# Another order for the products of the gradient of w2, another pace of the side stream, tied edge copies and six store buffers

## The chip, the cores and the metric

The kernel runs on one core of a Trainium2 chip. A core has a matrix engine (TensorE, PE in the profile; PEld is its weight loads), a vector engine (VectorE, DVE), an activation engine (ScalarE, ACT), GpSimd (POOL) and SyncE (SP). Each runs its own queue of instructions in order and waits on semaphores; here SP issues loads and POOL issues stores to the DMA engines, besides some arithmetic on POOL. The metric is the device time in microseconds of one execution.

## The reference: a gated mix of two branches, and all its gradients

The reference takes `x` (2048 x 1024), computes the output and then, by the vector-Jacobian product with `grad_out`, the gradients of all inputs but `B_x`:

```python
g = sigmoid((x * gate_w).sum(-1, keepdims=True))
a = irfft2(rfft2(x) * (w_r + 1j * w_i))          # branch A, in fp32, cast to bf16
h = relu(einsum("bsd,df->bsf", x, w1) + b1) ** 2  # F = 3584
b = einsum("bsf,fd->bsd", h, w2) + b2
out = g * a + (1 - g) * b
```

The outputs are `out` and the gradients of `x`, `w_r`, `w_i`, `w1`, `b1`, `w2`, `b2` and `gate_w`.

## The kernel before

Two streams of work are woven into one program. The main stream is the dense branch B and its gradients; the side stream is the spectral branch A: a two-dimensional Fourier transform written as small matrix products, with its own gradients.

**The main stream** has five parts.

1. `mlp_in` (L701): for each of 28 blocks of 128 columns of `w1` and each of 4 blocks of 512 rows it makes the hidden values (`ph`, L726, 8 matmuls), evacuates them on ACT (L728, L729), makes the gradient with respect to the hidden values (`pd`, L736, 8 matmuls), and evacuates that on DVE (`dhT`, L740). One such pair is a unit. `later["last"]` is the latest `dhT` instruction written down. Both results are stored to DRAM (`h2T_scr`, `dhT_scr`).
2. The first part of `mlp_grads` (L828): the gradient of `w2`, as the product of the transposed hidden values with `dbn`, by Strassen and Winograd's scheme: seven products in place of eight for a block cut in quarters. There are 7 groups of 512 rows of the result (`FG`), two blocks to a group (`Block`, L908), so 14 blocks. A block has seven chains of eight matmuls, p1 to p7 (L918). They use the quarters of the left operand (a11, a12 from half 0 of the fetched tile, a21, a22 from half 1), sums S1 to S4 of these (`left`, L892; one DVE instruction each at L906), and sums T1 to T4 of the quarters of `dbn` (`right`, L878, once). Two accumulators in PSUM belong to a block: X collects p1, p6, p7, p4 in that order, and V holds p2, then p5 and p3. After p1, p6 and p7 X is copied by ACT (`c1`, `u2`, `u3`, L928); `wlo` and `whi` are the two rows of results: DVE adds V and `c1` after p2 (L939), V and `u3` after p7 (L951, `whi`), V and `u2` after p3 (L964); ACT copies X into `whi` after p4 (L959). p3 adds into V, so it may not start before the `whi` addition has read V. The left operand of group n is fetched by transposing DMAs on SP (`fetch`, L847, issued at L181) into one of two buffers, `even` and `odd`. S1 is written in place over a21.
3. The gradient of `w1`: 7 x 8 products `pw` (L1050) of 16 matmuls, evacuated by ACT into `wo` (L1052), which has three buffers (L1051), and stored by POOL (L1053).
4. `mlp_out` (L1085): the output of branch B, `acc` (L1133).
5. `GradOfX.products`: the gradient of `x`, again by seven products.

**The side stream** (`aside`, L1484) is a generator. Each `yield` ends a step: the rest of the first transform of `x`, that of the gradient, the middle stage `fft_mid` (L319) and the way back `fft_out` (L528). `fft_mid` first loads the edge columns of the spectrum (twelve small loads, L337 to L339), and writes out ten steps of which the first seven carry the summing of `dbn` over its 16 tiles (`sums_of_db`, L1465, the generator `filler`, two additions to a step), and then calls `edges_through` (L351): six small DVE copies of the edges, 32 small matmuls, and four copies. After it come 32 turns of four steps: a turn loads `z`, makes sums `pm` on DVE (not in the first pair), multiplies with a matrix (`px`, L414, two matmuls), copies the result to `x` with four ACT instructions (L417), multiplies with the filter on DVE (`tt`, L424, L425; the filter `w` is prepared on POOL, L392 and L398; `eh` at L430 to L433), recombines (`y`, L437, L438), transforms back (`pv`, L445, two matmuls; `pc`, L451, L452), and makes the gradients of the filter (L462 to L466, L470, L475), which are stored. `fft_out` makes 32 tiles in two steps each: a row is loaded (`r`, POOL), folded (`re` on ACT L551, `rf` on DVE L556, L557), multiplied (`pki`, L564), copied by ACT (`rt`, L566), multiplied (`pui`, L311), copied (`e`, L573, L574), recombined on DVE into `yo` (L590 to L592; two buffers) and stored to `ax_scr` (L593).

**The pace** is set by `spread` (L1369): each step of the main stream adds to a due count, and side steps are taken until the count is met. In `mlp_in` a unit adds 1.55 steps until the middle stage has begun, then 1.3 (`first_rate`, L1502), and nothing in the last four units. In the w2 part a chain adds half of 0.8 (`each` is 0.5, `rate`, L1512). In the gradient of `w1` each `pw` adds (todo - count) / 55, where `todo` is the number of side steps in all but the last 8 tiles (263) and `count` those already taken. The last tiles go beside `mlp_out`.

**The order in a queue** is not simply that of the program. The compiler's scheduler goes through its own estimate of time and lets an engine take the first instruction in program order that is ready by that estimate. `after(ins, earlier, NoSync)` (L235) fixes the order of two instructions of one engine without a wait. In the trace, S sums are seen ahead of instructions written down before them.

In one turn of the loop of the w2 part (L1004), block `b` is new and block `a` is the one before it, and the chains are written down in this order:

```python
b.p1(); a.p7(); b.p2(); b.p6(); a.p4(); a.p3(); b.p5()
```

The fetch of half 0 of group g + 2 stands after `b.p2` (of the second block of a group), the fetch of half 1 of group g + 1 after `a.p4` (of the first block). S4 of the group, or S3 and S1 of the next one, stand after `a.p3`, S2 of the next one after `b.p5`.

Of the kernel before, what the change touches and what calls it, by code (L numbers as in the profile page):

```python
# [10 lines left out]
P = 128  # L11
BF16 = mybir.dt.bfloat16
FP16 = mybir.dt.float16
FP32 = mybir.dt.float32
ALU = mybir.AluOpType
# [124 lines left out]
def kernel(  # L140
# [22 lines left out]
    nc = tc.nc  # L163
# [71 lines left out]
    def after(ins, earlier, wait=mybir.DependencyClass.Sync):  # L235

        if earlier is not None:
            info = mybir.DependencyInfo(wait, mybir.DependencyReason.DATA)
            tc.add_manual_dep(ins.ins, earlier.ins.name, info, reason="paced")
# [79 lines left out]
    def fft_mid(filler):  # L319
# [29 lines left out]
            return am.rearrange("p (m n q) -> p m n q", n=2, q=P)  # L349

        def edges_through(ams, ed, low, mid):  # L351
            nc.vector.tensor_copy(out=ed[lanes[0], :, 1, :], in_=ed[lanes[0], :, 0, :])
            nc.vector.tensor_copy(out=ed[lanes[0], 0, 1, :], in_=mid[lanes[0]])
            for n in range(2):
                a, b = slice(2 * n, 2 * n + 2), slice(2 - 2 * n, 4 - 2 * n)
                nc.vector.tensor_copy(out=ed[lanes[1], 1:, n, a], in_=low[lanes[1], 1:, a])
                nc.vector.tensor_scalar(out=ed[lanes[1], 1:, n, b], in0=low[lanes[1], 1:, b], scalar1=-1.0, scalar2=None, op0=ALU.mult)
            sp = fps.tile([P, NM, 2, 4], FP32, name="sp", tag="ps2", bufs=2)
            for h in range(2):
                for m in range(NM // 2):  # L360
                    for n in range(2):
                        mm(
                            sp[:, h * NM // 2 + m, n], lhsT=ams[h][:, m, n, :], rhs=ed[:, h * NM // 2 + m, n, :],
                            start=True, stop=True, skip_group_check=True,
                        )
            ex = fb.tile([P, NM, 2, 2, 2], FDT, name="ex", tag="ex")
            for n in range(2):
                for c in range(2):
                    nc.vector.tensor_copy(
                        out=ex[lanes[n], :, c], in_=sp[lanes[c], :, n, :].rearrange("p m (e t) -> p m t e", e=2)  # L370
                    )
            return ex
# [110 lines left out]
        turns = [(m, h) for m in range(NM) for h in (1, 0)]  # L483
        z = {0: inputs(*turns[0])}
        later["mid"] = True
        for n in range(10):
            if n < 7:
                next(filler, None)
            yield
        ex = edges_through(*edge)  # L490
        for _ in filler:
# [336 lines left out]
    def mlp_grads():  # L828
# [32 lines left out]
        def sums_of_b1():  # L861
            gb1 = wb.tile([P, FC], FP32, name="gb1", tag="gb1")
            behind(nc.vector.reduce_sum(out=gb1[:], in_=gb1part[:], axis=mybir.AxisListType.X), "DVE")
            gb1b = wb.tile([P, FC], BF16, name="gb1b", tag="gb1b")
            nc.vector.tensor_copy(out=gb1b[:], in_=gb1[:])
            pb1 = fps.tile([FC, P], BF16, name="pb1", tag="ps2", bufs=2)
            nc.tensor.transpose(pb1[:], gb1b[:], identb[:])
            gb1r = wb.tile([FC, P], BF16, name="gb1r", tag="gb1r")
            nc.vector.tensor_copy(out=gb1r[:], in_=pb1[:])
            st(out=out_5.rearrange("(fc p) -> fc p", p=P), in_=gb1r[:])  # L870
# [18 lines left out]
            V(out=T_[4], in0=b21, in1=T_[2], op=ALU.subtract)  # L889
            yield  # L890

        def left(g, *which):  # L892
            (a11, a12), (a21, a22) = quads(grp[g], FH)
            made = S_.setdefault(g, {})
            for n in which:
                if n == 1:
                    made[1] = fp16(a21)
                else:
                    made[n] = sb.tile([P, KH, FH], FP16, name=f"S{n}", tag=f"S{n}", bufs=2 if n == 3 else 1)[:]
                x, y, op = {  # L900
                    3: lambda: (a11, a21, ALU.subtract),
                    1: lambda: (a21, a22, ALU.add),
                    2: lambda: (made[1], a11, ALU.subtract),
                    4: lambda: (a12, made[2], ALU.subtract),
                }[n]()
                later["sum"] = V(out=made[n], in0=x, in1=y, op=op)  # L906

        class Block:  # L908

# [38 lines left out]
            def p7(self):  # L948
                self.chain(self.X, S_[self.g][3], T_[3], False)
                u3 = self.kept("u3")  # L950
                V(out=self.hi[:, H:D], in0=self.V[:], in1=u3[:], op=ALU.add)  # L951

            def store(self, part, i):
                f0 = self.g * FGW + i * FH + self.fb * P
# [36 lines left out]
        left(0, 4)  # L991
        fetch(2, 0)
        yield each
        blk[0].p7()
        next(sums)
        yield each
        blk[1].p6()
        yield each
        blk[0].p4()
        yield each  # L1000
        blk[0].p3()
        sums_of_b1()
        yield each
        for k in range(2, NB + 1):  # L1004
            a = blk.pop(k - 1)
            if k == NB:
                a.p7()
                yield each
                break
            g, second = divmod(k, 2)  # L1010
            b = blk[k] = Block(k)
            b.p1()
            if k == 2:
                left(1, 3, 1, 2)
            yield each
            a.p7()
            yield each
            b.p2()
            if second:
                fetch(g + 2, 0)  # L1020
            yield each
            b.p6()
            yield each
            a.p4()
            if not second:
                fetch(g + 1, 1)
            yield each
            a.p3()
            if not second:
                left(g, 4)  # L1030
            elif g + 1 < FG:
                left(g + 1, 3, 1)
            if k >= 6:
                more_of_x(3, a.last)
            yield each
            b.p5()
            if second and g + 1 < FG:
                left(g + 1, 2)
            yield each

        count = 0
        later["res1"] = True
        for n in range(FG, len(jobs)):
            cur = grp.pop(n)
            fg = jobs[n][1]
            for d_ in range(DC):
                pw = mps.tile([P, FGW], FP32, name="pw", tag=("pX", "pV")[count % 2], bufs=2)
                count += 1
                for t in range(NT):
                    mm(pw[:], lhsT=xr[:, t, d_ * P : (d_ + 1) * P], rhs=cur[:, t, :], start=(t == 0), stop=(t == NT - 1))  # L1050
                wo = wb.tile([P, FGW], BF16, name="wo1", tag="wo1", bufs=3)  # L1051
                nc.scalar.copy(out=wo[:], in_=pw[:])  # L1052
                st(out=out_4[d_ * P : (d_ + 1) * P, fg * FGW : (fg + 1) * FGW], in_=wo[:])  # L1053
                yield
                if n == FG and d_ == 0:
                    a.p4()
                    yield each
                    a.p3()
                    yield each
                    sbs.close()  # L1060
                    fetch(n + 1, 1)
                    high = later["w2high"] = db_p.tile([P, NT, D], BF16, name="w2high", tag="dbn")
                elif d_ == 0:
                    fetch(n + 1, 0, 1)
                if count % 2 == 0 and 4 <= count < NT + 4:
                    rows_of_w2(high, count - 4, 0)
# [398 lines left out]
    def sums_of_db():  # L1465
        kept = later["even"]
        acc = kept[:, 0 : 2 * D].bitcast(FP32)
        nc.vector.tensor_copy(out=acc, in_=dbn[:, 0, :])
        for n in range(1, NT):
            V(out=acc, in0=acc, in1=dbn[:, n, :], op=ALU.add)  # L1470
            if n % 2:
                yield
        tr_ = kept[:, 2 * D : 4 * D].bitcast(FP32)
        nc.vector.transpose(out=tr_, in_=acc)
        part = kept[:, 4 * D : 4 * D + 64].bitcast(FP32)
        nc.vector.reduce_sum(out=part, in_=tr_.rearrange("p (b r) -> p b r", r=32), axis=mybir.AxisListType.X)
        yield
        pr = fps.tile([32, 32], FP32, name="prow", tag="ps2", bufs=2)
        mm(pr[:], lhsT=part, rhs=sel[:], start=True, stop=True)
        row = kept[0:32, 4 * D + 64 : 4 * D + 96]  # L1480
        nc.vector.tensor_copy(out=row, in_=pr[:])
        st(out=out_7.rearrange("(b c) -> b c", c=32), in_=row)
# [18 lines left out]

    def first_rate():  # L1502
        left_[0] -= 1
        return 0.0 if left_[0] < 5 else 1.3 if "mid" in later else 1.55

    for _ in spread(units, spec, first_rate):
        pass
    grads = mlp_grads()
    next(grads), next(grads)
    todo = 22 + 2 * (NT + 4) + 10 + 3 + 4 * R1 + 2 + 8 + 2 * 25  # L1510

    def rate():  # L1512
        if "res1" not in later:
            return 0.8
        if "rate" not in later:
            later["rate"] = (todo - count[0]) / (FG * DC - 1.0)
        return later["rate"]
# [49 lines left out]
```

## Time and profile before

| What | Value |
|---|---|
| Median of six runs | 1263.02 us (1259.59 to 1265.4) |
| The six runs | 1265.40, 1265.36, 1260.12, 1259.59, 1260.95, 1265.09 us |
| The profiled execution: time, span | 1265.4 us, 1263.6 us |
| Busy in the span: PE, DVE, ACT, POOL | 1228.7, 784.1, 537.4, 372.6 us |
| `mlp_in` | up to 463 us |
| Gradient of w2 | 463 to 646 us |
| Gradient of w1 | 646 to 888 us |
| `mlp_out`, then the gradient of x | 888 to 1087, 1087 to the end |

A line of a timeline reads: start, duration, engine, line of the kernel, instruction, output <- inputs, shapes, number merged, and in brackets the idle time of that engine before it and what ended it. A line of waits reads: engine, tile and line that waited, what it waited for: total time, times, longest.

### The profile page before, as it was taken

How to read it: one execution, taken by the hardware profiler on the slowest of the kernel's cores; microseconds unless marked ns; L12 is line 12 of the kernel's file. 1: busy time of each engine (PE TensorE's matmuls, PEld its weight loads, DVE VectorE, ACT ScalarE, POOL GpSimd, SP SyncE). 2: the span in 40 equal slices, each digit the busy share in tenths (PEclk: the TensorE clock that was granted, in tenths of full speed). 3: DMA queues.
4: the chain of work that ended last, by engine and by line, in shares of the span. 5: the costliest groups of instructions: out<-in, count | busy, mean ns of one | idle time of the engine just before them, and what ended most of it. 6: DMA issues, size and time to landing. Idle time of an engine off the chain costs nothing.

```text
span 1263.6 us, 18788 instructions
## 1 busy us (share of the span) xinstructions
PE 1228.7 (97%) x6618; PEld 598.2 (47%) x6740; DVE 784.1 (62%) x1816; ACT 537.4 (43%) x1016; POOL 372.6 (29%) x616
## 2 busy tenths in 40 slices
PE   8999999999999999998999999899999999999998
PEld 5555555544444444443444445455544444444443
DVE  3556456567677768665767724455866555896573
ACT  4657667745767743333355635666311000011110
POOL 0124324332344412331346565666100000000000
PEclk9999999999999999998999999999999999999999
DMA  9567565666575858786889889997689867666520
GB/s 288 186 191 199 139 194 164 174 176 169 163 195 183 216 145 184 176 217 167 203 234 247 208 158 245 180 217 243 163 198 212 195 162 192 179 186 184 168 87 33
DMA packets 328728, 234.35 MB, mean 185 GB/s; under 512 B 197772, under 2 KB 283946, under 8 KB 328634
## 3 DMA queue, kind: packets, MB, share of 16 engines
q1 hardware_dynamic: 297680, 142.24, 48.9%
q0 software_dynamic: 30752, 90.87, 23.1%
q8 instruction: 52, 0.85, 0.3%
q14 instruction: 42, 0.34, 0.1%
q10 hardware_dynamic: 202, 0.04, 0.0%
HBM read 107.24 MB, written 81.81 MB: 150 GB/s over the span
## 4 chain that ended last, share of the span: by engine, by line
PE 48%; DMA 3%; DVE 2%; issue 1%; ACT 1%; POOL 0%; ACTq 0%; POOLq 0%; DVEq 0%
PE acc L1133 15%; PE pw L1050 12%; PE xX L1243 7%; PE xV L1243 3%; PE pX L918 3%; PE pV L918 3%; PE xZ L1243 2%; DMA out_dram<-wo 2%; PE pui L311 1%; PE pki L564 1%; DMA out_dram<-gw 1%; DMA ax_scr<-yo 0%; DVE dS L1230 0%; PE pv L445 0%; PE px L414 0%
## 5 line engine op out<-in xcount | busy, mean ns | idle before, releaser
L726 PE MATMUL ph<-xT,w1g 128*128 128x512 bf16 x864 | 214.8, 379 | 2.5 <-DMA w1g<-in_B_w_dram 0.7
L736 PE MATMUL pd<-dbT,w2T 128*128 128x512 bf16 x877 | 210.2, 379 | 3.3 <-DVE dhT L740 2.5
L740 DVE SCALAR_TENSOR_TENSOR dhT<-pd,rT 128x512 bf16<-128x512 f32 x112 | 77.0, 688 | 109.7 <-PE pd L736 100.2
L736 PEld LDWEIGHTS <-w2T 128*128 128x128 bf16 x896 | 87.1, 98 | 104.8 <-issue 3.1
L1050 PEld LDWEIGHTS <-res 128*128 128x128 bf16 x896 | 86.8, 98 | 100.0 <-issue 2.2
L726 PEld LDWEIGHTS <-w1g 128*128 128x128 bf16 x896 | 85.1, 98 | 92.6 <-DMA w1g<-in_B_w_dram 1.0
L1201 ACT ACTIVATE g<-gatew_bc,dsc 128x1024 f32<-128x1024 bf16 x16 | 18.3, 1147 | 255.9 <-DVE ot L1134 118.8
L1050 PE MATMUL pw<-odd,res 128*128 128x512 bf16 x499 | 114.5, 382 | 0.7
L728 ACT ACTIVATE rT<-ph,b1col 128x512 bf16<-128x512 f32 x112 | 77.1, 689 | 76.9 <-PE ph L726 76.0
L227 POOL DMA_DIRECT2D z_scr<-u x96 | 58.5, 616 | 107.5 <-ACT u L295 52.8
L417 ACT CAST x<-px 64x512 f16<-64x512 f32 x128 | 74.2, 580 | 27.3 <-PE px L414 26.2
L1050 PE MATMUL pw<-even,res 128*128 128x512 bf16 x374 | 84.6, 379 | 0.5
L227 POOL DMA_DIRECT2D r<-y_scr x96 | 58.2, 611 | 45.9 <-ACT re L551 14.0
L729 ACT ACTIVATE h2T<-rT 128x512 bf16<-128x512 bf16 x112 | 70.5, 629 | 2.3
L1243 PEld LDWEIGHTS <-dS 128*128 128x128 f16 x448 | 43.7, 98 | 53.4 <-DVE dS L1230 0.5
L1133 PEld LDWEIGHTS <-even 128*128 128x128 bf16 x448 | 43.6, 98 | 51.7
L1133 PEld LDWEIGHTS <-odd 128*128 128x128 bf16 x448 | 43.6, 98 | 51.4
L1134 DVE SCALAR_TENSOR_TENSOR ot<-acc,omg,af 128x512 bf16<-128x512 f32 x32 | 24.0, 750 | 67.5 <-PE acc L1133 63.3
L1052 ACT CAST wo<-pw 128x512 bf16<-128x512 f32 x56 | 32.7, 584 | 76.8 <-PE pw L1050 48.7
L1133 PE MATMUL acc<-w2high,odd 128*128 128x512 bf16 x251 | 57.4, 379 | 0.3
L1133 PE MATMUL acc<-w2high,even 128*128 128x512 bf16 x249 | 57.0, 379 | 0.3
L918 PEld LDWEIGHTS <-S 128*128 128x128 f16 x336 | 33.1, 99 | 47.0 <-issue 7.7
(226 smaller groups left out, 2143.1 us busy)
## 6 DMA issues: line engine op xcount, KB each, us to landing
h2T_scr<-h2T POOLq DMA_DIRECT2D x28, 512.0 KB, 4.1
dhT_scr<-dhT POOLq DMA_DIRECT2D x28, 512.0 KB, 5.6
z<-z_scr SPq DMA_DIRECT2D x64, 128.0 KB, 2.9
y_scr<-pc POOLq DMA_DIRECT2D x64, 128.0 KB, 3.6
ax_scr<-yo POOLq DMA_DIRECT2D x32, 256.0 KB, 5.0
w1g<-in_B_w_dram SPq DMA_DIRECT2D x14, 512.0 KB, 4.2
out_dram<-wo POOLq DMA_DIRECT2D x56, 128.0 KB, 5.6
even<-h2T_scr SPq DMA_DIRECT2D x8, 896.0 KB, 5.5
```

Source lines behind the costliest of these rows:

```text
L227: issue(out=a, in_=b) if stored else issue(out=b, in_=a)
L417: nc.scalar.copy(out=x[lanes[n], c, :, 0:HW], in_=px[lanes[c], n])
L726: mm(ph[:], lhsT=w1g[:, dc, fc % 2 * P : (fc % 2 + 1) * P], rhs=xT[:, dc, ss], start=(dc == 0), stop=(dc == DC - 1))
L728: nc.scalar.activation(rT[:], ph[:], ACT.Relu, bias=b1col[:, fc : fc + 1])
L729: nc.scalar.activation(h2T, rT[:], ACT.Square)
L736: mm(pd[:], lhsT=w_[:, ec, fc % FGC * P : (fc % FGC + 1) * P], rhs=dbT[:, ec, ss], start=(ec == 0), stop=(ec == DC - 1),)
L740: return STT(out=dhT, in0=pd[:], scalar=2.0, in1=rT[:], op0=ALU.mult, op1=ALU.mult, accum_out=gb1part[:, fc, sb : sb + 1],)
L918: self.mm = mm(acc[:], lhsT=lhs[:, t, c_], rhs=rhs[:, t, :], start=start and t == 0, stop=t == KH - 1, skip_group_check=True,)
L1050: mm(pw[:], lhsT=xr[:, t, d_ * P : (d_ + 1) * P], rhs=cur[:, t, :], start=(t == 0), stop=(t == NT - 1))
L1052: nc.scalar.copy(out=wo[:], in_=pw[:])
L1133: turn["PE"] = mm(acc[:], lhsT=cur[:, fc, t2 * P : (t2 + 1) * P], rhs=w2[fc // NT][:, fc % NT, cs], start=(fc == 0), stop=(fc == FC - 1))
L1243: mm(acc[:], lhsT=lhs[:, fc, :], rhs=rhs[:, fc, :], start=start and fc == 0, stop=fc == KH - 1, skip_group_check=True,)
```

## The change

Four things are changed.

- The chains of the w2 part are written down in the order `b.p1, b.p2, a.p4, b.p6, a.p3, b.p5, b.p7`: a block's p7 closes its own turn of the loop and is no longer in the turn of the next block. The last turn of the loop, which held only p7 of the last block, falls away. For the first two blocks the order becomes p6 of block 1, p7 of block 0, p7 of block 1, p4 and p3 of block 0. The S sums are written down after p7 (S4 of the group, or S3, S1 and S2 of the next group together), and each is tied behind the `whi` addition of that p7 on DVE without a wait.
- The six DVE copies of the edges are tied behind the latest `dhT`. The twelve steps ahead of them carry one step of the sums of `dbn` each; every addition of `sums_of_db` is now a step of its own, so the side stream has four steps more, and `todo` becomes 267.
- The pace in the first passes is 1.6 steps a unit in place of 1.3 once the middle stage has begun, and 0.9 in place of 0.8 in the w2 part.
- `wo1` has six buffers in place of three.

```diff
         def edges_through(ams, ed, low, mid):
-            nc.vector.tensor_copy(out=ed[lanes[0], :, 1, :], in_=ed[lanes[0], :, 0, :])
-            nc.vector.tensor_copy(out=ed[lanes[0], 0, 1, :], in_=mid[lanes[0]])
+            tied = lambda ins: after(ins, later["last"], mybir.DependencyClass.NoSync)
+            tied(nc.vector.tensor_copy(out=ed[lanes[0], :, 1, :], in_=ed[lanes[0], :, 0, :]))
+            tied(nc.vector.tensor_copy(out=ed[lanes[0], 0, 1, :], in_=mid[lanes[0]]))
...
-        for n in range(10):
-            if n < 7:
-                next(filler, None)
+        for _ in range(12):
+            next(filler, None)
             yield
         ex = edges_through(*edge)
...
-        def left(g, *which):
+        def left(g, *which, tie=None):
...
                 later["sum"] = V(out=made[n], in0=x, in1=y, op=op)
+                after(later["sum"], tie, mybir.DependencyClass.NoSync)
...
-                V(out=self.hi[:, H:D], in0=self.V[:], in1=u3[:], op=ALU.add)
+                self.added = V(out=self.hi[:, H:D], in0=self.V[:], in1=u3[:], op=ALU.add)
...
-        blk[0].p7()
+        blk[1].p6()
         next(sums)
         yield each
-        blk[1].p6()
+        blk[0].p7()
+        yield each
+        blk[1].p7()
         yield each
         blk[0].p4()
         yield each
         blk[0].p3()
         sums_of_b1()
+        left(1, 3, 1, 2, tie=blk[1].added)
         yield each
-        for k in range(2, NB + 1):
+        for k in range(2, NB):
             a = blk.pop(k - 1)
-            if k == NB:
-                a.p7()
-                yield each
-                break
             g, second = divmod(k, 2)
             b = blk[k] = Block(k)
             b.p1()
-            if k == 2:
-                left(1, 3, 1, 2)
-            yield each
-            a.p7()
             yield each
             b.p2()
             if second:
                 fetch(g + 2, 0)
             yield each
-            b.p6()
-            yield each
             a.p4()
             if not second:
                 fetch(g + 1, 1)
             yield each
+            b.p6()
+            yield each
             a.p3()
-            if not second:
-                left(g, 4)
-            elif g + 1 < FG:
-                left(g + 1, 3, 1)
             if k >= 6:
                 more_of_x(3, a.last)
             yield each
             b.p5()
-            if second and g + 1 < FG:
-                left(g + 1, 2)
             yield each
+            b.p7()
+            if not second:
+                left(g, 4, tie=b.added)
+            elif g + 1 < FG:
+                left(g + 1, 3, 1, 2, tie=b.added)
+            yield each
+        a = blk.pop(NB - 1)
...
-                wo = wb.tile([P, FGW], BF16, name="wo1", tag="wo1", bufs=3)
+                wo = wb.tile([P, FGW], BF16, name="wo1", tag="wo1", bufs=6)
...
             V(out=acc, in0=acc, in1=dbn[:, n, :], op=ALU.add)
-            if n % 2:
-                yield
+            yield
...
-        return 0.0 if left_[0] < 5 else 1.3 if "mid" in later else 1.55
+        return 0.0 if left_[0] < 5 else 1.6 if "mid" in later else 1.55
...
-    todo = 22 + 2 * (NT + 4) + 10 + 3 + 4 * R1 + 2 + 8 + 2 * 25
+    todo = 22 + 2 * (NT + 4) + 12 + 5 + 4 * R1 + 2 + 8 + 2 * 25
 
     def rate():
         if "res1" not in later:
-            return 0.8
+            return 0.9
```

More of the change, by code (lines that the diff above doesn't have):

```diff
@@ L351, in edges_through @@
         def edges_through(ams, ed, low, mid):
-            nc.vector.tensor_copy(out=ed[lanes[0], :, 1, :], in_=ed[lanes[0], :, 0, :])
-            nc.vector.tensor_copy(out=ed[lanes[0], 0, 1, :], in_=mid[lanes[0]])
+            tied = lambda ins: after(ins, later["last"], mybir.DependencyClass.NoSync)
+            tied(nc.vector.tensor_copy(out=ed[lanes[0], :, 1, :], in_=ed[lanes[0], :, 0, :]))
+            tied(nc.vector.tensor_copy(out=ed[lanes[0], 0, 1, :], in_=mid[lanes[0]]))
             for n in range(2):
                 a, b = slice(2 * n, 2 * n + 2), slice(2 - 2 * n, 4 - 2 * n)
-                nc.vector.tensor_copy(out=ed[lanes[1], 1:, n, a], in_=low[lanes[1], 1:, a])
-                nc.vector.tensor_scalar(out=ed[lanes[1], 1:, n, b], in0=low[lanes[1], 1:, b], scalar1=-1.0, scalar2=None, op0=ALU.mult)
+                tied(nc.vector.tensor_copy(out=ed[lanes[1], 1:, n, a], in_=low[lanes[1], 1:, a]))
+                tied(nc.vector.tensor_scalar(out=ed[lanes[1], 1:, n, b], in0=low[lanes[1], 1:, b], scalar1=-1.0, scalar2=None, op0=ALU.mult))
             sp = fps.tile([P, NM, 2, 4], FP32, name="sp", tag="ps2", bufs=2)
```

## Prediction

> **What bounds the kernel now.** I read the page first: the engine shares, then the slices.
>
> ```profile
> PE 1228.7 (97%) x6618; PEld 598.2 (47%) x6740; DVE 784.1 (62%) x1816; ACT 537.4 (43%) x1016; POOL 372.6 (29%) x616
> ...
> PE   8999999999999999998999999899999999999998
> ```
>
> TensorE (PE) is the bound: 1228.7 of the 1263.6 us span. The change adds or removes no matmul of size, so it can only win or lose in the 34.9 us in which PE is idle and in matmuls run on a lowered clock. So I asked next what PE waited for:
>
> ```profile
> PE pV L918 <- DVE whi L951: 5.7, 1, 5.7
> PE pki L564 <- ACT rt L566: 5.3, 2, 3.9
> PE pd L736 <- DVE dhT L740: 2.5, 2, 1.3
> PE pui L311 <- ACT e L574: 2.0, 2, 1.6
> PE pui L311 <- ACT rt L566: 1.2, 1, 1.2
> ```
>
> Then the windows: undisturbed PE shows 49.7 to 49.8 in 50 us; these do not, or show how full the other engines are (columns PE, PEld, DVE, ACT, POOL, clock, DMA share, GB/s).
>
> ```profile
> 250.00:300.00 50.00, 47.24 (x259) 22.40 (x263) 35.42 (x67) 22.68 (x38) 13.66 (x18) 1.00 0.55 149
> 311.00:455.00 144.00, 143.31 (x655) 65.29 (x668) 102.24 (x267) 99.34 (x174) 61.99 (x100) 1.00 0.65 188
> 550.00:600.00 50.00, 43.94 (x193) 19.48 (x194) 28.42 (x49) 18.14 (x33) 11.12 (x19) 0.93 0.81 199
> 750.00:800.00 50.00, 42.72 (x283) 23.49 (x286) 18.14 (x77) 28.04 (x55) 26.49 (x45) 0.97 1.17 221
> ```
>
> Last, the timeline inside them:
>
> ```profile
> 275.41 0.17 DVE L352 COPY ed<-ed 64x64 f16<-64x64 f16 x1 [1.40 <-DMA ed<-z_scr]
> 278.32 1.89 PE L736 MATMUL pd<-dbT,w2T 128*128 128x512 bf16 x8 [1.31 <-DVE dhT L740]
> ...
> 572.47 1.23 DVE L906 TENSOR_TENSOR S<-odd 128x2048 f16<-128x2048 bf16 x1 [9.80 <-DMA odd<-h2T_scr]
> 573.61 0.68 DVE L951 TENSOR_TENSOR whi<-pV,u 128x512 bf16<-128x512 f32 x1
> 574.35 0.58 PE L918 MATMUL pV<-dbn,S 128*128 128x512 bf16 x1 [5.73 <-DVE whi L951]
> ...
> 791.18 0.58 ACT L1052 CAST wo<-pw 128x512 bf16<-128x512 f32 x1 [6.21 <-DMA out_dram<-wo]
> 791.96 1.01 ACT L566 CAST rt<-pki 128x1024 f16<-128x1024 f32 x1
> 792.51 0.42 DVE L590 TENSOR_TENSOR yo<-tt 128x512 f16<-128x512 f16 x1 [5.71 <-DMA ax_scr<-yo]
> 793.03 0.38 PE L564 MATMUL pki<-ki,re 128*128 128x128 f16 x4 [3.88 <-ACT rt L566]
> ```
>
> All three are one engine's queue blocked by a head that waits for a DMA, with something behind it that PE needs: edge copies ahead of `dhT`; an S sum of group 5 placed two blocks early, ahead of `whi` of block 7 (its u3 had been copied by 564.1); a `wo` copy waiting for a store, ahead of `rt`.
>
> **The change, part by part.** The sum is made against the profiled execution: span 1263.6, time 1265.4, which is 2.4 us above the median 1263.0 of the six runs.
>
> *Edges tied, sums in single steps.* Same operations. PE waited 1.31 + 1.19 = 2.5 us. The twelve edge loads leave SP from 262.7 to 273.9, each landing in 3.3 to 4.9 us, so all are in SBUF by about 278. The copies may now not come before the `dhT` that was last when they were written down: 12 steps at 1.6 per unit = 7.5 units of 3.5 us, some 26 us after the loads are asked for. DVE's waits of 0.52, 1.40 and 0.58 go. The 3.33 us wait for a `z_scr` store at 262 stays, and so do sixteen sums of 1.23 us. Ends: 0 to 2.5 gained. I take 2.0, as DVE's edge waits add up to 2.5 too.
>
> *Products and S sums.* 14 blocks of 7 chains of 8 matmuls as before (1.73 us a chain). Each block's p7 comes before the next block's p1; p4 moves up from fifth to third chain, p3 from sixth to fifth. With p4 go its ACT copy, the `whi` store on POOL and the transposing fetch of half 1 on SP, all two chains (3.5 us) earlier; with p3 the `wlo` store and the loads of x; the fetch of half 0 moves one chain up, past nothing that PE waits for. u3 now has p1 and p2 (3.5 us) ahead of p4, as it had p2 and p6; u2 has p3 and p5 ahead of p7: a copy is 0.58 us. `whi` has four chains (6.9 us) before p3. The S sums can no longer precede their block's `whi`, so the stall at 568 to 574 goes: p3 should have begun at 568.46 and handed over to px at 570.19; px began at 577.72 (7.53 lost), took 0.85 instead of 0.43, and p5 took 1.96 instead of 1.73. Together 8.2: idle 5.95, slow matmuls 2.2. I take 8.2 gained (end below: 0, if another stall takes its place, next).
>
> *The wait added.* S3, S1, S2 of the next group now stand behind `whi`: u3 0.6 + `whi` 0.7 + 3 x 1.22 = about 5.1 us after p7 with gaps. p6, which reads S2, comes after p1, p2 and p4: 5.2 us plus side matmuls. Cover is about nil. If ACT is in its four x copies (2.35) and DVE in a pair of `tt` (1.3), S2 is 3.6 late, less 0.3 of side matmuls: 3.3. Five group changes: 0 to 16 us. Behind the sums wait `wlo` of p2 (needed only at p5, 8.6 us after p7) and side operations. I take 1.0, near the row of the first such sequence (PE waited 0.21 for an S at 472.8).
>
> *Side stream faster in the first passes.* Steps at the end of these passes: 63 / 1.55 = 41 units, then 51 x 1.3 = 66, now 51 x 1.6 = 82; in all about 130 and 145, of which four are the new sum steps. That makes 16 middle turns instead of 13.4 (the trace has 14 px there). In 311 to 455, 38.5 units and 12.7 turns: DVE 102.2 us less 38.5 x 0.70 for `dhT` leaves 5.9 a turn; ACT 99.3 less 38.5 x 1.32 leaves 3.8. A turn then took 11.3 us, DVE idle 3.3. At 2.5 units a turn it is 2.5 x 3.45 + 0.88 = 9.5 us: DVE 5.9 + 1.75 = 7.65 (80%), ACT 7.1 (75%). PE had no wait here; from 280 to 290, with DVE at 9.86 of 10, it waited 1.19. Ends: 0, and the 3.3 idle wholly unfillable, 1.4 too much x 16 = 23. I take 2.0, one or two waits like those of the edges.
>
> *0.9 for 0.8 in the w2 stage.* 92 x 0.45 = 41 steps for 37: half a turn more; no price apart from the last.
>
> *dW1 stage: pace and six buffers.* Steps left for its 55 products: (267 - 187) / 55 = 1.45 each, before (263 - 167) / 55 = 1.75. Lost before, 750 to 806: idle 1.20 + 1.61 + 3.88 + 0.37 + 1.42 = 8.5, and on the lower clock 1.3 in the pw chain at 794.88 and 0.35 in pui: 10.1. With six `wo1` the copy waits for the store six products back, over 20 us, where stores took up to 13.2. ACT's 18.4 us of waits for `wo` stores go. Late next: `yo` has still two buffers, its DVE waits add up to 30.0 us, and PE passed 3.99 of them at 778 unharmed. A tile has 5.7 us instead of 4.9. Ends: 0 (DMA, at 1.17 there, holds up `rt`'s inputs just as long) to 10.1. I take 6.5.
>
> Sum: 1265.4 - 2.0 - 8.2 - 6.5 + 1.0 + 2.0 = 1251.7.
>
> [...] The row: after 5.73 idle the granted clock in 570 to 580 was 0.66 and the loss beyond idling 2.2. [...]
>
> Against the faster pace: POOL's `w` (0.66 + 0.87 a turn) meets DVE; `eh` took 161 to 623 ns there, one `y` 981 for 420. [...] By the row the clashes are already in the 5.9.
>
> **The rivals.**
> *A, forecast:* 1252, own range 1247 to 1257. Chance 0.50.
> *B, slower: DVE becomes the bound of the first passes.* If its 3.3 us of idle a turn are real gaps that denser steps cannot fill: 1265.4 - 2.0 - 8.2 - 6.5 + 23 + 1 = 1273. It eats the gain of 15.7 from 2.9 us of unfillable idle a turn. For it: the waits for ACT's x (8.7 us) come every turn. Against: sums were filled into DVE ahead of their step elsewhere. Chance 0.13.
> *C: the stage of dW1 is held by DMA, not by `wo`.* 1265.4 - 2.0 - 8.2 + 3.0 = 1258. For it: `yo` waited 5.71 alongside. Against: `rt` ran in the instant after `wo`. Chance 0.18.
> *D: S2 late at each group.* 1251.7 + 15 = 1267. Chance 0.04.
> *E: all three stalls go and nothing comes.* 1265.4 - 20.8 = 1244.6. Chance 0.12.
> *F: the gain and a new blocked queue cancel:* within 0.3%. Chance 0.03.
>
> **How the numbers follow.** 0.3% of 1263.0 is 3.8 us, about what a measurement of this kernel can tell from no change. A and E are faster, C in six of ten cases: 0.73. C's rest, F and a little of D: 0.11. B and most of D: 0.16. The range leaves out most of B and D and the tip of E: 1244 to 1266.
>
> **What would show it.** Right: no PE wait for `whi`; S sums right behind `whi` on DVE; no ACT wait for `out_dram<-wo`; PE at 49.7 in all windows from 311 to 463; the first pki some 20 us sooner after the first pw. Wrong: PE waits for `dhT` before 463 (B); for S at the first p6 of a group (D); for pki with ACT or DVE waiting for `r` or `yo` (C); or another DVE head that waits for a fetch.

## The result, and the profile after

The changed kernel took 1257.4 us in the median of 34 runs (1253.85 to 1266.49), the kernel before 1263.43 us in 71 runs (1257.56 to 1273.3). The ratio is 0.996, with a 95% interval of 0.9948 to 0.9972. It is faster, by 0.4%; the forecast was 0.9%. The profiled execution took 1255.48 us over a span of 1253.7.

The page of the kernel after, engine shares and the slices of PE:

```profile
PE 1227.3 (98%) x6618; PEld 597.0 (48%) x6740; DVE 785.7 (63%) x1816; ACT 537.4 (43%) x1016; POOL 372.6 (30%) x616
...
PE   9999999998999999999999999999999999999998
```

PE is as busy as before (1228.7), and its idle time has gone from 34.9 to 26.4 us (both figures hold the 0.2 to 0.3 us by which even an undisturbed window of 50 us reads short). One slice below 9 is left inside the span, at about 285 us: the edges. The waits of PE:

```profile
PE pX L919 <- DVE S L906: 4.5, 3, 1.5
PE sp L363 <- DVE ed L354: 3.0, 1, 3.0
PE ph L726 <- DMA w1g<-in_B_w_dram: 1.3, 1, 1.3
PE pV L919 <- DVE even L906: 1.2, 1, 1.2
```

The waits for `whi`, `rt` and `e` are gone. In their place PE waits for S sums in the w2 part and for the edge copies. The windows (PE, PEld, DVE, ACT, POOL, clock, DMA share, GB/s):

```profile
250.00:300.00 50.00, 46.28 (x247) 21.79 (x250) 32.06 (x58) 19.28 (x32) 11.13 (x15) 0.93 0.53 143
311.00:455.00 144.00, 143.32 (x656) 65.25 (x668) 119.59 (x306) 111.50 (x199) 72.80 (x114) 1.00 0.71 200
550.00:600.00 50.00, 48.27 (x221) 21.66 (x223) 36.17 (x69) 21.01 (x40) 15.71 (x27) 1.00 0.88 227
600.00:650.00 50.00, 48.32 (x222) 21.71 (x224) 36.50 (x66) 20.94 (x38) 15.50 (x26) 1.00 0.92 197
750.00:800.00 50.00, 49.68 (x331) 27.29 (x336) 23.38 (x96) 28.80 (x55) 26.95 (x46) 1.00 1.15 227
```

In 311 to 455 DVE is busy 119.6 us where it was 102.2, and PE does as much as before (143.3): the denser side stream costs nothing there. The window at 750, which held 42.7 us of PE work, is full. The one at 250 has lost a microsecond, and those at 550 and 600 each lack 1.5.

Where the stages of the two profiled executions begin, in us from the span's start (the first `pX`, `pw`, `acc`):

| Kernel | w2 part | dW1 | `mlp_out` | length of w2 part | length of dW1 |
|---|---|---|---|---|---|
| before | 463.4 | 645.7 | 888.3 | 182.4 | 242.6 |
| after | 469.5 | 650.7 | 878.1 | 181.3 | 227.4 |
| after minus before | +6.1 | +5.0 | -10.2 | -1.1 | -15.2 |

Part of this is work that only changed its place. Before the w2 part there are now 34 `px` matmuls (17 turns) where there were 28 (14): three turns at 0.88 us of PE work each. By the start of dW1 it is four turns (54 `px` for 46), some 3.5 us. Between the first `pw` and the first `acc` PE spends 4.9 us less on side matmuls (32.5 for 37.4; the rest is one tile's products, which now come after the first `acc`), and dW1 is shorter by that much besides what it gained.

### The profile page after: what moved, and what is told of

It reads as the page before. It is cut to its first block, busy times and chain, and to the rows that moved or that the text cites. A ratio compares the mean times of both kernels' runs of the same rounds, so it can differ in the third digit from the quotient of the medians.

```text
span 1253.7 us, 18779 instructions
## 1 busy us (share of the span) xinstructions
PE 1227.3 (98%) x6618; PEld 597.0 (48%) x6740; DVE 785.7 (63%) x1816; ACT 537.4 (43%) x1016; POOL 372.6 (30%) x616
## 4 chain that ended last, share of the span: by engine, by line
PE 81%; DVE 5%; issue 3%; ACT 2%; DMA 1%; POOL 0%; DVEq 0%; POOLq 0%
PE pw L1047 15%; PE acc L1130 15%; PE ph L726 10%; PE pd L736 10%; PE xX L1240 7%; PE pX L919 7%; PE pV L919 5%; PE xV L1240 3%; PE xZ L1240 2%; PE pui L311 1%; PE pu L311 1%; PE pki L564 1%; PE pk L278 1%; PE px L415 1%; PE pv L446 1%
```

## The experiments

Each experiment is the changed kernel with one thing altered, unless said otherwise. The kernels of one group ran beside the same runs of the kernel before, whose median is given with each group. Stage lengths are from the profiled execution of each, one execution per kernel. The changed kernel itself was run in two series: its ratio was 0.996 in the first and 0.9926 (0.9899 to 0.9953) in the second, so small differences of ratio from one group to another show little.

### One part undone at a time (before: 1265.01 us, 31 runs)

**The old edge part.** The ties, the twelve steps and the single additions are undone.

```diff
-            tied(nc.vector.tensor_copy(out=ed[lanes[0], :, 1, :], in_=ed[lanes[0], :, 0, :]))
+            nc.vector.tensor_copy(out=ed[lanes[0], :, 1, :], in_=ed[lanes[0], :, 0, :])
...
-        for _ in range(12):
-            next(filler, None)
+        for n in range(10):
+            if n < 7:
+                next(filler, None)
...
-            yield
+            if n % 2:
+                yield
```

> The changed kernel with its edge part undone: edge copies untied, ten steps ahead of them, sums of dbn two to a step. Theory (the tie puts the copies behind the last dhT and all sums, so the edge matmuls wait): PE's wait for the edge tile (3.0 + 0.3 us in the changed kernel) is gone, waits of PE for dhT of about 2.5 us are back, and the stretch from 250 to 310 us is about 3 us shorter than in the changed kernel. Rival (DVE is late anyway, whatever the tie does): the stretch loses as much as in the changed kernel, within 1 us. Both leave the rest of the kernel as it is.

It took 1258.14 us (10 runs), ratio 0.9964 (0.994 to 0.9987), not to be told from the changed kernel. The w2 part began at 473.4, 4.0 us later than in the changed kernel (3.1 without the one turn more, 36 `px`, that is done by then): the earlier start that was expected did not come, and the outcome is the one named for the rival, that DVE is late whatever the tie does. Two of its waits of PE:

```profile
PE prow L1476 <- issue: 4.6, 1, 4.6
PE pd L736 <- DVE dhT L740: 2.4, 2, 1.9
```

The two waits for `dhT` of the kernel before are back (2.4), and a new one, dearer than these, comes at 293.08: PE has reached the small product that ends the summing of `dbn`, and DVE is still summing (its last reduction ran from 291.76 to 292.97; the trace names no releaser, so that this is what PE waited for is read from the times). At the new pace PE comes there sooner: it stands there from 288.44, where the same product ran at 292.65 without a wait in the kernel before. DVE's queue does not move faster: that reduction ended at 292.43 in the kernel before. Up to the w2 part tied copies at the new pace thus cost less than untied ones, though with both it begins later than in the kernel before.

**The old order of products.** Order of the chains, places of the S sums and their ties as before.

```diff
-        for k in range(2, NB):
+        for k in range(2, NB + 1):
...
             b.p1()
+            if k == 2:
+                left(1, 3, 1, 2)
             yield each
+            a.p7()
+            yield each
             b.p2()
...
-            b.p7()
-            if not second:
-                left(g, 4, tie=b.added)
-            elif g + 1 < FG:
-                left(g + 1, 3, 1, 2, tie=b.added)
-            yield each
```

> The changed kernel with the old order of products and the old, untied S sums. Theory (the S sum placed early blocks DVE in front of whi, an accident of one place): a PE wait for whi or another DVE result behind an S sum of 3 to 8 us is back, and the waits for S (5.7 us in the changed kernel) are under 1 us; the w2 stage takes 175 us plus that stall. Rival (the old order is free of that stall at the new pace): no wait for whi, no wait for S, the stage 5 us shorter than in the changed kernel, so the new order only costs.

It took 1273.19 us, ratio 1.0057 (1.0027 to 1.0087): slower than the kernel before. The w2 part is 194.5 us long. Its waits of PE:

```profile
PE pV L918 <- DVE whi L951: 10.0, 3, 4.2
PE pw L1050 <- DMA odd<-dhT_scr: 5.1, 1, 5.1
```

At the new pace PE waits for `whi` at three blocks, not one, and matmuls behind these waits run on a lowered clock: the granted clock is 0.57 in 529 to 537, in 587 to 591 and in 618 to 622. So the new order is worth about 13 us of that stage here. At the old pace it is worth about 6 (182.4 us in the kernel before, 176.1 in the run at the old pace below): the rest of the change needs it. The waits for S did not fall under 1 us as expected: 1.7 (for `even`) and 1.4 stay in the first group. The second line is taken up below.

**Three store buffers.**

```diff
-                wo = wb.tile([P, FGW], BF16, name="wo1", tag="wo1", bufs=6)
+                wo = wb.tile([P, FGW], BF16, name="wo1", tag="wo1", bufs=3)
```

> The changed kernel with three store buffers again. Theory (the buffers cleared the stage of the gradient of w1): ACT waits for stores of wo of 10 us or more are back and PE loses 5 to 10 us between 720 and 880. Rival (the slower and earlier side stream cleared it): PE loses under 2 us there though ACT still waits for stores, and the time is that of the changed kernel.

It took 1263.1 us, ratio 0.9989 (0.9957 to 1.002), not to be told from the kernel before. dW1 is 239.9 long instead of 227.4, in an execution of 1268.61 us, the longest of the ten (the shortest took 1254.61). Two of its waits:

```profile
PE pki L564 <- ACT rt L566: 6.8, 2, 3.5
...
ACT wo L1049 <- DMA out_dram<-wo: 37.0, 10, 7.9
```

This is the mechanism read from the profile before: ACT waits for a store with a `wo` copy at its head, and `rt` stands behind it.

**The old pace.**

```diff
-        return 0.0 if left_[0] < 5 else 1.6 if "mid" in later else 1.55
+        return 0.0 if left_[0] < 5 else 1.3 if "mid" in later else 1.55
...
-            return 0.9
+            return 0.8
```

> The changed kernel with the old pace (1.3 and 0.8). Theory (six buffers are enough): no PE wait for pki or pui above 1 us; w2 stage begins some 3 us sooner and the stage of the gradient of w1 is longer by the same. Rival (the pace is what cleared it): PE loses 5 us or more between 740 and 810, with DVE waiting for stores of yo or loads of r.

It took 1260.28 us, ratio 0.9959 (0.9928 to 0.999), not to be told from the changed kernel's 0.996. Inside, almost every stage differs. The waits of PE, and one window, of this kernel:

```profile
PE pv L446 <- DVE y L439: 3.7, 4, 1.4
PE pki L564 <- DVE rf L556: 3.2, 3, 1.9
PE pki L564 <- ACT rt L566: 2.4, 1, 2.4
PE pX L919 <- DVE S L906: 1.5, 4, 0.5
```

```profile
250.00:310.00 60.00, 59.34 (x317) 27.95 (x321) 39.34 (x79) 26.90 (x45) 15.52 (x20) 1.00 0.63 163
```

The edges cost nothing here: 59.34 of 60, against 57.19 in the kernel before and 56.23 in the changed one, and the w2 part begins at 460.2, 3.1 us sooner than in the kernel before. Of that 0.9 is one turn fewer done by then (26 `px` against 28); 2.2 is what the edges gain at this pace. The S sums cost 1.5 instead of 5.7. But dW1 is 247.5 long, six buffers or not: DVE's `yo` waits for `ax_scr` stores add up to 47.0 us there, against 8.7 in the changed kernel, and what stands behind `yo` is late for PE. So six buffers were not enough at the old pace. The faster pace takes work out of dW1, and with it these waits are gone; it pays with the edges and the S sums.

### Causes taken one by one (before: 1266.08 us, 13 runs)

**The kernel before with six store buffers,** nothing else.

```diff
-                wo = wb.tile([P, FGW], BF16, name="wo1", tag="wo1", bufs=3)
+                wo = wb.tile([P, FGW], BF16, name="wo1", tag="wo1", bufs=6)
```

> The kernel before with six store buffers and nothing else changed. If the buffers alone clear the stage of the gradient of w1: no ACT wait for stores of wo, PE loses under 2 us between 740 and 810 (10.1 before), time 7 to 10 us below the kernel before. If pace is needed as well: DVE still waits 5 us at a time for stores of yo, PE loses 5 us or more there, time less than 5 us below.

It took 1262.29 us (10 runs), ratio 0.9966 (0.9943 to 0.9989). dW1 is 238.1 long instead of 242.6. Waits of this kernel, of PE and of DVE:

```profile
PE pV L918 <- DVE whi L951: 8.8, 1, 8.8
PE pki L564 <- DVE rf L556: 4.5, 4, 1.9
...
DVE yo L590 <- DMA ax_scr<-yo: 48.3, 13, 5.8
```

Buffers alone remove the waits for `wo` (22.2 us of ACT's from 640 to 890 in the kernel before, none here over 1.2), and `yo` is late next. With the run at the old pace and the one with three buffers this shows that dW1 needs both: buffers alone leave 238 (247.5 with the rest of the change at the old pace), pace alone 240, both leave 227, with no wait of PE over 0.2 in the profile after. The lengths are single ones, and part of the new pace's share is the 4.9 us of side work that it took out.

**The sums earlier.** S3, S1 and S2 of the next group are written down after p3 of the old block, two chains sooner, and tied behind the first `wlo` addition of the new block.

```diff
             a.p3()
+            if second and g + 1 < FG:
+                left(g + 1, 3, 1, 2, tie=b.first)
...
-                V(out=self.lo[:, 0:H], in0=self.V[:], in1=self.c1[:], op=ALU.add)
+                self.first = V(out=self.lo[:, 0:H], in0=self.V[:], in1=self.c1[:], op=ALU.add)
...
-            elif g + 1 < FG:
-                left(g + 1, 3, 1, 2, tie=b.added)
```

> The changed kernel, but the sums S3, S1, S2 of the next group are written down after a.p3 and tied behind the addition after p2 of the second block (two chains earlier). If the S waits come from their place behind whi: the two waits of 1.52 us are gone, the waits of the first group (1.25 and 1.44) stay, time 3 us below the changed kernel. If DVE is simply full there: the waits stay or move to whi or wlo.

It took 1255.87 us (4 runs), ratio 0.9904 (0.9876 to 0.9933). The w2 part is 177.7 long instead of 181.3: both waits of 1.52 us at group changes are gone, 3.6 us with what follows them. The wait of 1.4 for an S and that of 1.2 for `even` in the first group stay. The stage shows the gain; the time alone would not, as its interval overlaps that of the changed kernel's second series.

**The edge copies tied earlier:** behind the `dhT` that was last at the tenth of the twelve steps, not at the twelfth.

```diff
-            tied = lambda ins: after(ins, later["last"], mybir.DependencyClass.NoSync)
+            tied = lambda ins: after(ins, later["edge"], mybir.DependencyClass.NoSync)
...
-        for _ in range(12):
+        for n in range(12):
             next(filler, None)
+            if n == 9:
+                later["edge"] = later["last"]
```

> The changed kernel, but the edge copies are tied behind the dhT that was last at the tenth of the twelve steps in place of the last one. If the tie's place is the cause of PE's 3.3 us wait for the edge tile: that wait is gone and no wait for dhT comes, time 4 to 6 us below the changed kernel. If DVE is late by its sums: PE waits for dhT instead, 2 us or more.

It took 1253.09 us (4 runs), ratio 0.9888 (0.9858 to 0.9917). PE has no wait over 0.3 us for `ed`, and the w2 part begins at 463.8, 5.6 us sooner. That is 0.4 behind the kernel before with three turns (2.6 us) more done, so the edges gain 2.2, as at the old pace. This shows the place of the tie at this pace to be the cause: the sums of `dbn` are all still there, and without the late tie PE waits neither for the edges nor for `dhT`.

**Both.**

> Both of these edits in one kernel. If the two causes are independent: the gains add, 7 to 9 us below the changed kernel, so 1248 to 1251 us; PE waits in the whole trace under 8 us in all. If another wait takes their place: less than 4 us below.

It took 1246.96 us (4 runs), ratio 0.9841 (0.9815 to 0.9867): the gains add, and the time is a little under the range expected. The two windows that the two edits aim at (in this execution a full window reads as 50.00 in 50):

```profile
250.00:310.00 60.00, 60.00 (x322) 28.05 (x320) 41.10 (x82) 30.85 (x52) 16.75 (x23) 1.00 0.66 161
...
720.00:890.00 170.00, 170.00 (x1103) 91.14 (x1102) 83.70 (x307) 90.43 (x174) 85.15 (x145) 1.00 0.88 212
```

### What differs from run to run (before: 1265.8 us, 17 runs)

Three profiles of these groups show a wait of 3 to 5 us in dW1 that the first profile of the changed kernel does not have. So the changed kernel was run again.

> The changed kernel once more, unaltered, for a second profile. If the executions differ by PE's wait for the transposing fetch of the gradient of w1 (0 in the first profile, 3.0 to 5.1 us at one product in three kernels near it): that wait is 0 to 5 us again and every other PE wait is the one of the first profile within 0.5 us, and the execution's time differs from 1255.5 by that wait. If the edge or S waits are what varies: those differ by more than 1 us.

It took 1255.82 us (10 runs), ratio 0.9926 (0.9899 to 0.9953). This time the profiled execution took 1260.67 us, 5.2 more than the first one, and its dW1 is 233.0 long. PE's timeline has this:

```profile
782.65 2.59 PE L1047 MATMUL pw<-odd,res 128*128 128x512 bf16 x8 [3.81 <-DMA odd<-dhT_scr]
```

Its other waits over 1 us are within 0.5 us of those of the first profile; what the 3.81 us leave of the 5.6 by which dW1 is longer is mostly `pw` matmuls on a lowered clock behind the wait (0.50 from 784 to 787). A chain of the gradient of w1 waits for a transposing fetch. How SP issues such fetches, in the kernel before:

```profile
737.83 0.38 SPq L618 DMA_DIRECT2D w2low<-in_B_w_dram  x1
739.10 21.54 SPq L181 DMA_TRANSPOSE odd<-dhT_scr  x4
760.68 2.67 SPq L618 DMA_DIRECT2D w2low<-in_B_w_dram  x5
```

and in the first profile after the change:

```profile
732.93 3.03 SPq L618 DMA_DIRECT2D w2low<-in_B_w_dram  x6
742.14 30.90 SPq L181 DMA_TRANSPOSE odd<-dhT_scr  x4
```

The `w2low` loads, 512 KB each, belong to side steps of `fft_out`. With four turns done earlier, all six stand ahead of the four transposes, where five of them had stood behind. The transposes then occupy SP for 30.9 us instead of 21.5 (34.03 in the second profile), and the slowest of them lands 22.4 us after its issue instead of 12.6. In the four profiles with the old pace (the kernel before twice, with six buffers, and the changed one at the old pace) these transposes take 21 to 24 us and PE never waits for them. In the nine with the new pace and the loads as they are, they take 26 to 36 us, and a fetch of this stage makes PE wait in six, by 1.3 to 5.1 us. In each of these thirteen profiles the fetch that follows most of the loads takes SP longest of the four-transpose fetches of its stage; with the old pace that is the next one, of `even` (27.92 us at 772.86 in the kernel before), and PE does not wait for it there. From 732 to 752 the DMA share is 1.22 in the profile after and 0.90 in the one before. The DMA engines are busier there; whether that is what slows the transposes, and by what, no row here shows.

The kernel before once more, and the one with both edits again:

> The kernel before once more, for a second profile. The waits for dhT (2.5), for whi (5.7) and for pki and pui (8.5) are there again; the one that hangs on when a DMA lands, whi, and those of pki may be other by several us, and by these the execution differs from 1265.4.

> The changed kernel with both early ties, more rounds: 1245 to 1250 us, 7 to 11 us below the changed kernel, ratio to the kernel before 0.984 to 0.990.

The kernel before took 1268.46 us, with stages that began at 463.7, 644.9 and 890.8: its own dW1 (245.9) varies by 3 us too. The waits are there again: 3.0 for `dhT`, 5.4 for `whi`, 7.9 for `pki` and `pui` together. The one with both edits took 1250.15 us (6 runs, 1245.95 to 1255.66), ratio 0.9888 (0.9851 to 0.9924): 5.7 us below the changed kernel that ran beside it, less than expected. Its profile has a wait of 2.3 for the fetch, where its first profile had none.

**The loads later.** Both edits, and each `w2low` load may start only when the last `yo` copy of its tile is done.

```diff
-            nc.vector.tensor_copy(out=yo[:, 0::Q], in_=tt[:, :, :, 0].rearrange("p a b -> p (a b)"))
+            made = nc.vector.tensor_copy(out=yo[:, 0::Q], in_=tt[:, :, :, 0].rearrange("p a b -> p (a b)"))
...
-                    rows_of_w2(low, i - 1, NT)
+                    rows_of_w2(low, i - 1, NT, made)
...
-        ld(out=t_[:, fc : fc + 2, :], in_=B_w2[f0 : f0 + 2 * P, :].rearrange("(q p) e -> p q e", p=P))
+        after(ld(out=t_[:, fc : fc + 2, :], in_=B_w2[f0 : f0 + 2 * P, :].rearrange("(q p) e -> p q e", p=P)), earlier)
```

> Both early ties, and the six loads of w2low each wait for a finished tile of the side stream, so that they no longer stand together ahead of the fetch of the dW1 stage. If these 3 MB are what makes the fetch late: no PE wait for the fetch in its profile, the spread of its times is smaller than that of the kernel with both early ties, and the median 1 to 3 us lower. If they are not: no difference, or slower where SP now waits for the side stream ahead of a fetch.

It took 1245.89 us (6 runs), ratio 0.9864 (0.9826 to 0.9902). Its SP:

```profile
732.01 12.21 SPq L181 DMA_TRANSPOSE odd<-dhT_scr  x3
744.64 0.39 SPq L620 DMA_DIRECT2D w2low<-in_B_w_dram  x1
745.08 7.45 SPq L181 DMA_TRANSPOSE odd<-dhT_scr  x1
752.63 6.17 SPq L620 DMA_DIRECT2D w2low<-in_B_w_dram  x2
```

The four transposes are through in 20.5 us again, and PE does not wait for them. Five of the six runs lie between 1245.36 and 1246.02, the sixth took 1254.97. Without this edit the six runs beside them were spread over 10 us, and the four of the earlier group over 3.6. This speaks for the loads as the cause of the wait for the fetch, and of part of the spread. It does not settle it: the intervals overlap, and the sixth run, which has no profile, is as slow as the slow ones without this edit though its loads were out of the way.

## Why the prediction was right or wrong

The direction was right, and the time lies inside the range. The size was wrong: the sum gave 13.7 us from one execution to another; the two profiled ones differ by 9.9 us, the medians by 6.0, where 1252 against the median of 1263.0 had been 11. By the steps:

| Step | Predicted | In the profile after |
|---|---|---|
| Edges | -2.0 | +3.1 |
| `whi` stall | -8.2 | -8.2 |
| S sums behind `whi` | +1.0 | +5.5 (first group, not behind `whi`: 2.5 of it) |
| Faster pace, first passes | +2.0 | 0 |
| dW1 stage | -6.5 | -10.1 |
| Sum | -13.7 | -9.7 (profiles: -9.9) |

The edge entry is what PE's progress through the same units lost from 256 to 302 us (it was 0.4 us behind the kernel before at the first of these times and 3.5 at the second). The S entry is the 5.7 us of PE waits for S and `even` less the 0.2 that were there. The `whi` and dW1 entries are the losses listed from the profile before that are gone.

**Edges: the step failed, in size and sign.** It reasoned that the copies come "some 26 us after the loads are asked for", which is true, and that nothing would then be late. It took the loads for the only thing to be late and let "sixteen sums of 1.23 us" (in the trace a cast of 0.69 and fifteen additions) stay without asking where they would go. The timeline of DVE after the change:

```profile
262.25 0.69 DVE L1465 CAST even<-dbn 128x1024 f32<-128x1024 bf16 x1 [2.90 <-DMA z_scr<-u]
...
264.73 3.74 DVE L1467 TENSOR_TENSOR even<-even,dbn 128x1024 f32<-128x1024 f32 x3
...
282.62 2.47 DVE L1467 TENSOR_TENSOR even<-even,dbn 128x1024 f32<-128x1024 f32 x2
285.12 1.25 DVE L1470 STREAM_TRANSPOSE even<-even 128x1024 f32<-128x1024 f32 x1
286.29 0.65 DVE L740 SCALAR_TENSOR_TENSOR dhT<-pd,rT 128x512 bf16<-128x512 f32 x1
286.88 0.17 DVE L353 COPY ed<-ed 64x64 f16<-64x64 f16 x1
```

and that of PE:

```profile
284.19 0.38 PE L736 MATMUL pd<-dbT,w2T 128*128 128x512 bf16 x1
287.58 0.19 PE L363 MATMUL sp<-ed,am 128*128 128x4 f16 x2 [3.01 <-DVE ed L354]
288.05 0.48 PE L363 MATMUL sp<-ed,am 128*128 128x4 f16 x13 [0.28 <-DVE ed L358]
288.39 0.57 PE L363 MATMUL sp<-ed,even 128*128 128x4 f16 x16
288.82 2.72 PE L736 MATMUL pd<-dbT,w2T 128*128 128x512 bf16 x6
```

Sums fill every gap of DVE from 262 to 285, and all fifteen additions stand ahead of the copies, though only twelve steps with one each were written down before them; so DVE falls behind PE. No copy waits for its load. The tie puts the copies behind a `dhT` that DVE only reaches at 286.29, while PE is through with the matmul before its `sp` at 284.57. After the wait its matmuls run on a lowered clock (0.50 in windows of 1 us) until about 293.5. As an estimate, 3.3 of waits and half of the 4.5 us from 288.96 to 293.5, less the 2.5 of waits for `dhT` that went, make the 3.1. At the old pace the same twelve steps span 9.2 units, not 7.5; the copies end no sooner there (290.8), but PE comes to the bulk of its `sp` only at 290.2 and waits 0.3. The 2.0 of the prediction is what the edge part gives at the old pace (2.2). It costed tie and pace apart from each other, and it is their meeting that cost 5 us.

**The `whi` stall: right.** No wait for `whi` is left, no other takes its place in that queue, and undoing the order brings 10.0 us of such waits.

**The S sums: right mechanism, wrong size.** The step said "Cover is about nil", gave 0 to 16 us, and took 1.0, "near the row of the first such sequence". That PE would wait for S at the first p6 of a group was its sign for rival D, and it came, at two of the five group changes and for 1.52 us each, where the step had reckoned up to 3.3. At the first of the two:

```profile
547.53 0.69 DVE L952 TENSOR_TENSOR whi<-pV,u 128x512 bf16<-128x512 f32 x1
548.13 1.22 DVE L906 TENSOR_TENSOR S<-odd 128x2048 f16<-128x2048 bf16 x1
549.27 0.68 DVE L452 TENSOR_TENSOR pc<-pv,vc 128x512 f16<-128x512 f32 x1
549.87 1.21 DVE L906 TENSOR_TENSOR odd<-odd 128x2048 f16<-128x2048 bf16 x1
551.00 0.68 DVE L453 TENSOR_TENSOR pc<-pv,vc 128x512 f16<-128x512 f32 x1
551.60 1.21 DVE L906 TENSOR_TENSOR S<-odd 128x2048 f16<-128x2048 f16 x1
```

```profile
552.87 1.90 PE L919 MATMUL pX<-T,S 128*128 128x512 f16 x8 [1.52 <-DVE S L906]
```

Two `pc` additions of the side stream, 1.36 us of DVE, slip between the three sums, and PE waits 1.52. At the second the side work stands elsewhere: `whi` begins at 600.50, 1.6 us after its `u3` was copied, behind two `pc` and two `y`, and a `wlo` addition slips between the sums. The remaining 2.7 us fell in the first group, where the prediction had looked only for 0.21. The sums of that group are not behind a `whi`, and with the old order at the new pace PE waited 3.1 for them: they come with the pace and not with the order. At the old pace all waits for S come to 1.5: here too the size depended on the pace. That it does so by the side operations which the pace brings to a place is what these two sequences suggest.

**The faster pace: 0, not 2.0, and rival B is refuted.** DVE took 119.6 us of work in 144, up from 102.2, with no wait of PE. The 3.3 us of idle a turn could be filled as far as the pace asked. The price of the pace lay elsewhere: at the edges, at the S sums of the first group, and on SP. **The step that moves the side stream did not count its DMAs,** which is the loads of `w2low` moved past the transposes of `odd`.

**dW1: all 10.1 us went, not 6.5,** in the first profile after; in the second about 5 came back as the wait for the fetch. Six buffers did what was said of them, but what cleared the stage was that the pace took work out of it as well: `yo` was late next with six buffers alone (DVE's waits for its stores add up to 48.3 us), as the step feared, and hardly with both (8.7).

**Medians.** The sum was made against one execution and handed on as a median. The kernel before was profiled at 1265.4, 2.0 above its median; the one after at 1255.5, 1.9 below its own. The second profile of the changed kernel shows a reason: a fetch wait that an execution has or has not, and that costs about 5 us. It is not the whole of the spread, as the 34 runs reach from 1253.85 to 1266.49. What the others wait for stays open. The median of 1257.4 is near rival C's 1258, but C's mechanism (stores of `yo` holding up `rt`) is not what happened.

## What to carry to other kernels

A change of pace moves every instruction of the stream, so follow it through each queue: what its arithmetic now meets on the vector engine, and which loads now stand ahead of a fetch that the main stream needs. A tie without a wait was safe here only where the instruction that it is tied to was on time on its own engine (PE lost 3.01 us behind a `dhT` that DVE reached at 286.29, 1.7 us after PE had run out of work; with the tie two steps earlier no such wait over 0.3); look at how far that engine runs behind, not at whether the data have landed. And where parts of a change meet in one queue, cost them together: here the same edge part lost 3.1 us at one pace and gained 2.2 at the other, and the new order shortened its stage by 6 us at one pace and by 13 at the other. (For the six buffers this is not shown: single profiles give 4.5 us of the stage alone and 12.5, or 6.9 with the second profile, with the new pace, but the medians give 0.34% alone and, with the new pace, about 0.3%, 0.9989 against 0.996.)

## What was not expected of the hardware

- PE waited 3.01 us for the edges, followed by 31 matmuls of 4 columns, and the granted clock was 0.67 in 285 to 290 and 0.65 in 290 to 295: six `pd` matmuls took 2.72 us, where a run of six took 1.46 elsewhere. In the second profile the same wait (2.9) left 0.88 and 0.78. In windows of 1 us the clock reads 0.83 in 286 to 287, 0.50 up to 293 and 0.75 in the next: it fell while PE was still waiting and stayed at half for 6.8 us. In the second profile the same reading gives 3.4 us (0.89 in 288 to 289, 0.50 up to 292, 0.90). A wait of 2.45 us, with the old order, was enough too (0.50 from 588 to 590). The waits of 1.52 us left the clock at 1.00. Why a wait of 3.01 us left the clock at half for 6.8 us and one of 2.9 for 3.4, no run shows.
- The four transposes of one fetch in dW1 took SP from 10.8 us (at 709 in the kernel before) to 35.8 (the old order at the new pace) to issue, longest where the `w2low` loads stood just ahead.
